# Three moves in the first block of a one-core retention and Mish kernel: outer products ahead of scores, two weight casts to other engines, three weight sums later

## The chip, the cores and the metric

The kernel runs on one core of one Trainium2 chip. The metric is the device time of one execution, in microseconds (us); where several runs are compared, their median. The engines are called as the profile calls them: PE is TensorE's matmul row and PEld its weight loads, DVE is VectorE, ACT is ScalarE, POOL is GpSimd, SP is SyncE, which here only issues DMAs.

## The reference

There are two stages. The first is a linear recurrence for each batch and head (4 batches, 8 heads, 768 tokens, 64 wide), the second a feed-forward layer on its output (3072 tokens, 512 wide, 2048 inside):

```
state = gamma[h] * state + outer(k[t], v[t])      # 64x64 for each batch and head
y[t]  = scale * q[t] @ state
x     = y, heads side by side                     # 3072 x 512
h     = x @ w_in                                  # 512 x 2048
g     = h * tanh(softplus(h))                     # Mish
out   = g @ w_out                                 # 2048 x 512
```

All inputs and the output are float32; the kernel computes its matmuls in float16.

## The kernel before

**The recurrence in chunks.** The kernel cuts the tokens into 24 chunks of 128. Within a chunk the recurrence is a masked product: scores (k times q, L314 and L497), a mask (L321, L504, L565), and the product of the masked scores with v (the "present" part, L374). Between chunks it is a state: outer products of k and v (L333, L483) are added to the state so far and decayed (L345), and the state times q is the "past" part (L381). Both parts add up in PSUM and are copied out as `xt`, the transposed input of the second stage.

**Blocks.** The second stage works on blocks of chunks: the first block has 4 chunks (512 tokens), the other ten have 2 each. `first_block` is written out by hand: it holds the whole opening, in which inputs and weights arrive by DMA, and it is the function that the change edits, with `first_g2`, the second matmul of that block. From block 1 on, `g1_seven` (L820) and `seven` (L956) do the two matmuls with seven products in place of eight, which needs sums and differences of the weights (`win_sums`, L770, for w_in and `weight_sums`, L722 to L725, for w_out), of x (`x_sums`, L781 to L786) and of g (`g_sum`).

**Order of work.** The schedule is manual: every engine executes its instructions in the order in which the program issues them, and waits only on semaphores that the framework derives from the tiles. A list `late` holds closures for sums that aren't urgent; `some_late(n)` issues the next n of them at that place. `plan` says which extra work is issued behind the u-th group of the first block's first matmul (L687).

**The opening, chunks 2 and 3.** For this pair of chunks the program issues, in this order: the past part of chunk 1 (L381); the second halves of the scores and of the mask for the pair (L314, L321); the outer products of chunk 2 (L333) and its state (an identity matmul that adds the state so far, L343, and the decay, L345); the first-matmul groups u = 0 and 1 for the tokens of chunks 0 and 1 (L1057); the present part (L374), which reads the mask's output; the past parts of chunks 2 and 3 (L381), of which the last reads chunk 2's state; the cast of the second half of weight slice 0 (L206), and groups u = 2 and 3, which use that half.

**Weight slices.** w_in comes in four slices of 512 columns, each cast to float16 in two halves by `cast_win(s, half, engine)`: L206 on DVE or POOL, L204 on ACT. Slice 3 serves the groups u = 12 to 15; its second half serves u = 14 and 15.

**PSUM.** Two pools: `mm` has four buffers of one bank and `at` two buffers of two. The group u = 14 of L687 takes the `mm` buffer of group u = 10, which is free when ACT has computed the Mish of u = 10 (L703). At the start of block 1 (L820) the first two products on `mm` take the buffers of pair 0 of `first_g2`: the first is free after DVE's L1281, the third group of L820 (product "first", half 1) after ACT's L1286, which in the program waits for DVE's L1284. The product "fifth", half 0, waits for DVE's first L840.

**DVE and POOL in `first_g2`.** DVE's order there is: cast of w_out slice 2 (L216), L723, L724, L1183, L725, two L1247, L722, the fifth chunk's state L608, two masks L565, L723, L724, L1281, L725, L1284, then the sums of x. POOL's order is: a one-column copy that waits for L723 (`gate`, L427), two casts of q (L406), one of v (L423), two DMA issues (L418), two casts of v (L423), two DMA issues, a cast of q (L406).

Of the kernel before, what the change touches and what calls it, by code (L numbers as in the profile page):

```python
# [16 lines left out]
def kernel(  # L17
# [9 lines left out]
    nc = tc.nc  # L27
# [15 lines left out]
    NSL = 4  # L43
# [14 lines left out]
    def toks(c):  # L58
        return slice(c * HB, (c + 1) * HB)
# [83 lines left out]
    nload, late, early = [0], [], set()  # L143
    BRING = CPB
    stores = []
    last_ended, yet = [], []

# [49 lines left out]
    def cast_win(s, half, eng):  # L199
        src = wtmps["in", s]  # L200
        t = cpool.tile([P, NBP, TB // 2], FP16, name=f"win{s}_{half}")
        src = src[:, :, half * (TB // 2):(half + 1) * (TB // 2)]
        if eng is nc.scalar:
            nc.scalar.copy(t, src)  # L204
        else:
            eng.tensor_copy(t, src)  # L206
        wins[s, half] = t

    def cast_wout(s, f, on_act=False):
        if s not in wouts:  # L210
            wouts[s] = cpool.tile([P, FPS, d_model], FP16, name=f"wout{s}")
        dst, src = wouts[s][:, f], wtmps["out", s][:, f]
        if on_act:
            nc.scalar.copy(dst, src)
        else:
            nc.vector.tensor_copy(dst, src)  # L216
# [110 lines left out]
    def outer_first(s, chunks=(0, 1)):  # L327
        u_ps = {c: mmps.tile([P, HP, P], FP32, name="u_ps", tag="mm") for c in chunks}
        for i in range(HP):
            half, j = divmod(i, HP // 2)  # L330
            for r in range(R):
                for c in chunks:
                    nc.tensor.matmul(  # L333
                        u_ps[c][:, i], k16s[s][toks(c), half, r, 2 * j:2 * j + 2],
                        v16s[s, half][toks(c), r, 2 * j:2 * j + 2],
                        start=i == 0 and r == 0, stop=r == R - 1, skip_group_check=True)
        for c in chunks:
            us[2 * s + c] = u_ps[c]
# [46 lines left out]
    def xt_out(g, y):  # L385
        nc.scalar.copy(xts[0][:, g:g + 2], y)
# [47 lines left out]
    def at_tile():  # L434
        return atps.tile([P, 2, HP // 2, R, C], FP32, name="at", tag="at")
# [271 lines left out]
    def some_late(n):  # L707
        for _ in range(min(n, len(late))):
            late.pop(0)()
# [351 lines left out]
    def first_block():  # L1061
        qf = load_first_q()
        for s in range(2):
            for nm in "kv":
                for half in range(2):
                    load_two(nm, s, half)
        nload[0] = CPB
        load_weights()
        xts[0] = xtp.tile([P, CPB, HP, C], FP16, name="xt")

        at = at_tile()
        spin_wide(at, HP)
        spin_wide(at, HP)
        spin_wide(at, 2)
        tq = turn_first_q(qf, 0)
        spin(at, HP)
        first_q_out(0, tq, nc.scalar)
        tq = [tq, turn_first_q(qf, 1, True)]
        cast_two("k", 0, 0, True)
        turn_two(0, 0)  # L1080
        turned_two(0, 0)
        cast_two("k", 0, 1, True)
        turn_two(0, 1)
        first_q_out(1, tq[1], nc.vector)
        turned_two(0, 1)
        spin(at, HP)
        scores_half(0, 0, at)
        mask_half(0, 0, at)
        for half in range(2):
            cast_two("v", 0, half)  # L1090
        at = at_tile()
        spin(at, HP)
        scores_half(0, 1, at)
        mask_half(0, 1, at)
        cast_two("k", 1, 0)
        turn_two(1, 0)
        turned_two(1, 0)
        cast_two("k", 1, 1)
        outer_first(0)
        state_first(0)  # L1100
        at = at_tile()
        scores_half(1, 0, at)
        mask_half(1, 0, at)
        y = atps.tile([P, 2, HP, C], FP32, name="y_ps", tag="at")
        in_two = [y[:, c] for c in range(2)]
        present_first(0, in_two, range(HP))
        turn_two(1, 1)
        turned_two(1, 1)
        state_first(1)
        past_first(1, in_two)  # L1110
        xt_out(0, y)
        for half in range(2):
            cast_two("v", 1, half)
        cast_win(0, 0, nc.gpsimd)
        at = at_tile()
        scores_half(1, 1, at)
        mask_half(1, 1, at)
        y = [atps.tile([P, 2, HP, C], FP32, name="y_ps", tag="at")[:, 0] for _ in range(2)]
        outer_first(1, [0])
        state_first(2)  # L1120
        h_ps = [mmps.tile([P, 1, TB], FP32, name="h_ps", tag="mm") for _ in range(2)]
        for u in range(2):
            first_g1(h_ps[u], u, 0)
        present_first(1, y, range(HP))
        past_first(2, y)
        past_first(3, y)
        cast_win(0, 1, nc.vector)
        xt_out_by_two(2, y)
        for u in range(2, FPS):
            h_ps.append(mmps.tile([P, 1, TB], FP32, name="h_ps", tag="mm"))  # L1130
            first_g1(h_ps[u], u, 0)
        for u in range(FPS):
            first_g1(h_ps[u], u, 1)
            mish(0, u, h_ps[u])
        for s in range(1, NSL - 1):
            for half in range(2):
                cast_win(s, half, nc.vector)
            if s == 1:
                fourth_state()
            if s == 2:  # L1140
                late.extend(win_sums(0))
                some_late(8)
        room_for_sums()

        def more_sums():
            late.extend(win_sums(1))
            some_late(8)
            late.extend(weight_sums(0) + weight_sums(1))

        plan = {6: [(cast_win, NSL - 1, 0, nc.scalar)],  # L1150
                7: [(cast_win, NSL - 1, 1, nc.scalar), (more_sums,)],
                9: [(cast_wout, 0, slice(0, 3)), (cast_wout, 0, slice(3, 4), True), (room_for_more,),
                    (bring_first,)],
                10: [(some_late, 1)],
                12: [(g_sum, 1)],
                13: [(cast_wout, 1, slice(0, 3)), (g_sum, 2), (g_sum, 3)],
                16: [(load_more,)]}
        for u in range(FPS, NFB):
            g1(0, u)
            for fn, *args in plan.get(u + 1, ()):  # L1160
                fn(*args)
        first_g2()
        hsnaps.append(gp.tile([P, 4, TB], FP32, name="hsnap", tag="g0"))

# [20 lines left out]
    def first_g2():  # L1185
# [33 lines left out]
        for p in pairs:  # L1219
            mm(pe[p], sm(p, 1), t(1), True)  # L1220
            nc.scalar.copy(m5[p], pe[p])
        cast_wout(2, slice(0, 2))
        cast_wout(2, slice(2, 4), True)
        some_late(1)
        gate(tmats[0][:, 1, 0, :1])
# [28 lines left out]
        for p in pairs:  # L1254
            mm(px[p], a(p, 1, 1), b(1, 0))
            if p == 0:
                outer_fifth(CPB)
        cast_wout(3, slice(2, 4), True)
        decay_of_fifth()
        scores(CPB)  # L1260
# [158 lines left out]
```

## Time and profile before

| | us |
|---|---|
| median of 3 runs | 190.82 (190.69 to 191.54) |
| the profiled execution: its own time | 190.88 |
| the profiled execution: its span, first to last instruction | 189.0 |
| PE busy within the span | 182.5 |
| DVE busy | 155.6 |
| ACT busy | 126.8 |
| POOL busy | 95.3 |

The profile comes from one execution. Its span begins with the first instruction of the program and ends with the last; 1.9 us of the execution's time lie around it. A row of the timeline gives the start, the duration, the engine, the line of the kernel, the operation, its output and inputs, the shapes and the number of instructions merged into the row; in square brackets stands how long the engine was idle before it and what ended that idle time. Rows of pipelined instructions overlap a little.

### The profile page before, as it was taken

The page shows a single profiled execution, that of the slowest core. Times are in us where ns is not written, and L with a number is a line of the kernel's source. Part 1 is how long each engine was busy: PE and PEld are TensorE (multiplying, and loading weights), DVE is VectorE, ACT ScalarE, POOL GpSimd, SP SyncE. Part 2 cuts the span into 40 slices and gives each one's busy share as a digit, 9 for nine tenths or more (in the row PEclk, how much of TensorE's full clock was granted, in tenths as well). Part 3 has the DMA queues.
Part 4 walks back from the last instruction along what each step waited for, and adds up shares of the span by engine and source line. Part 5 has one row for each costly group of instructions (what it writes and reads, how often), then busy time and mean ns, then how long its engine had stood idle before and what let it go on. Part 6 is the DMA issues. An engine that isn't in the chain of part 4 may idle for free.

```text
span 189.0 us, 7724 instructions
## 1 busy us (share of the span) xinstructions
PE 182.5 (97%) x3283; PEld 155.8 (82%) x3283; DVE 155.6 (82%) x329; ACT 126.8 (67%) x249; POOL 95.3 (50%) x135
## 2 busy tenths in 40 slices
PE   7789999999999999999999999999999999999992
PEld 3457546975988988988988988988988989989981
DVE  3997899879899699797897897797897897796662
ACT  3462599385883983983983984974874974965960
POOL 6570107696878937924935925916916913000000
PEclk9999999999999999999999999999999999999999
DMA  5999999999999999999998995999996984300203
GB/s 165 351 368 405 404 407 279 278 248 134 151 192 251 180 285 210 208 219 177 167 194 146 188 187 158 197 195 120 178 203 117 148 144 59 114 0 17 101 0 111
DMA packets 95521, 36.17 MB, mean 191 GB/s; under 512 B 82560, under 2 KB 88960, under 8 KB 95488
## 3 DMA queue, kind: packets, MB, share of 16 engines
q1 hardware_dynamic: 74112, 32.78, 75.3%
q0 software_dynamic: 21088, 2.62, 22.4%
q8 instruction: 25, 0.41, 0.9%
q10 hardware_dynamic: 288, 0.30, 0.4%
q14 instruction: 8, 0.07, 0.1%
HBM read 27.30 MB, written 6.29 MB: 178 GB/s over the span
## 4 chain that ended last, share of the span: by engine, by line
PE 91%; DVE 3%; DMA 2%; POOL 1%; issue 1%; ACT 0%; SPq 0%; DVEq 0%; POOLq 0%
PE h_ps L820 34%; PE o_ps L956 32%; PE h_ps L687 6%; PE o_ps L1210 5%; DMA qfirst<-in_q_dram 2%; PE h_ps L1057 2%; PE o_ps L1275 2%; PE y_ps L532 2%; PE u_ps L483 2%; PE at L497 2%; DVE am L321 2%; PE y_ps L543 2%; POOL qfirst L249 1%; DVE osb L977 1%; PE at L314 0%
## 5 line engine op out<-in xcount | busy, mean ns | idle before, releaser
L840 DVE TENSOR_TENSOR hsum<-h_ps,hsnap 128x512 f32<-128x512 f32 x60 | 38.5, 685 | 10.1 <-ACT hsnap L830 6.6
L830 ACT COPY hsnap<-h_ps 128x512 f32<-128x512 f32 x60 | 32.1, 589 | 10.3 <-PE h_ps L820 10.1
L820 PEld LDWEIGHTS <-wsum 128*128 128x128 f16 x640 | 36.2, 98 | 0.1
L835 ACT ACTIVATE g<-hsum 128x512 f16<-128x512 f32 x60 | 34.6, 643 | 0.6 <-DVE hsum L840 0.2
L956 PEld LDWEIGHTS <-gsum 128*128 128x128 f16 x320 | 30.4, 98 | 3.7
L820 PE MATMUL h_ps<-xsum,wsum 128*128 128x128 f16 x480 | 30.2, 220 | 0.0
L956 PE MATMUL o_ps<-tmat,gsum 128*128 128x256 f16 x240 | 29.5, 273 | 0.0
L820 PEld LDWEIGHTS <-win 128*128 128x128 f16 x480 | 28.2, 98 | 0.9
L418 POOL DMA_DIRECT2D qk<-in_k_dram x36 | 27.5, 777 | 0.0
L956 PEld LDWEIGHTS <-g 128*128 128x128 f16 x248 | 22.7, 98 | 2.6
L406 POOL TENSOR_TENSOR qk<-qf,qvs 128x512 f16<-128x512 f32 x20 | 22.1, 1106 | 0.0
L956 PE MATMUL o_ps<-wout,g 128*128 128x256 f16 (+1 forms) x168 | 20.8, 268 | 0.0
L423 POOL TENSOR_TENSOR v<-vf,qvs 128x512 f16<-128x512 f32 x20 | 20.7, 1060 | 0.0
L820 PE MATMUL h_ps<-xt,win 128*128 128x128 f16 x320 | 19.6, 220 | 0.0
L550 ACT COPY hsum<-y_ps 128x512 f32<-128x512 f32 x9 | 5.3, 585 | 18.3 <-PE y_ps L543 18.3
L977 DVE TENSOR_TENSOR osb<-o_ps,snap 128x256 f32<-128x256 f32 (+1 forms) x32 | 13.0, 413 | 5.0 <-PE o_ps L956 2.4
L597 POOL TENSOR_TENSOR stc<-suc,gcv 128x256 f16<-128x256 f32 x15 | 9.9, 662 | 13.6 <-DVE suc L592 13.6
L427 POOL COPY gate<-gsum 128x1 f16<-128x1 f16 x10 | 1.9, 186 | 26.8 <-DVE gsum L927 26.8
L965 ACT COPY snap<-o_ps 128x256 f32<-128x256 f32 x31 | 11.4, 371 | 5.4 <-PE o_ps L956 5.0
L820 PE MATMUL h_ps<-xsum,win 128*128 128x128 f16 x160 | 12.3, 220 | 0.0
L820 PE MATMUL h_ps<-xt,wsum 128*128 128x128 f16 x160 | 12.2, 220 | 0.0
L835 ACT ACTIVATE g<-h_ps 128x512 f16<-128x512 f32 x20 | 12.0, 599 | 0.0
(144 smaller groups left out, 309.4 us busy)
## 6 DMA issues: line engine op xcount, KB each, us to landing
vf<-in_v_dram SPq DMA_DIRECT2D x24, 256.0 KB, 6.2
out_dram<-osb SPq DMA_DIRECT2D x22, 256.0 KB, 2.9
qf<-in_q_dram SPq DMA_DIRECT2D x20, 256.0 KB, 5.3
wi<-in_moe_w_in_dram SPq DMA_DIRECT2D x3, 1024.0 KB, 10.5
wt<-in_moe_w_out_dram SPq DMA_DIRECT2D x3, 1024.0 KB, 9.6
qk<-in_k_dram POOLq DMA_DIRECT2D x36, 64.0 KB, 5.1
qfirst<-in_q_dram SPq DMA_DIRECT2D x2, 512.0 KB, 4.3
kf<-in_k_dram SPq DMA_DIRECT2D x4, 256.0 KB, 4.9
```

What stands on the lines that cost most here:

```text
L406: nc.gpsimd.tensor_tensor(by_head(g, room16(g)[0]), by_head(0, loaded[g][0]), f.broadcast_to((P, 2, HP, D)), op=ALU.mult)
L418: nc.gpsimd.dma_start(room16(g)[1][:, x::2], src[:, HP * x:HP * x + HP])
L423: nc.gpsimd.tensor_tensor(room16(g)[2], loaded[g][2], vs.unsqueeze(2).broadcast_to((P, H, D)), op=ALU.mult)
L597: by.tensor_tensor(stcs[g], sus.pop(g), decay, op=ALU.mult)
L687: nc.tensor.matmul(h_ps[:, j], win(s, f, bp), xt(blk, bp), start=(bp == 0), stop=(bp == NBP - 1))
L820: nc.tensor.matmul(h_ps[g][:, f], w(g, f, d), x(d), start=first and f == 0 and d == 0, stop=d == n - 1, skip_group_check=True)
L830: nc.scalar.copy(x, h_ps)
L835: nc.scalar.activation(gt[:, fb:fb + FPS, j * P:(j + 1) * P], h, AF.Mish, scale=inv_boost3)
L840: nc.vector.tensor_tensor(h, h_ps, x, op=ALU.add)
L956: nc.tensor.matmul(t, x(f), w(f)[:, c], start=first and f == 0, stop=f == n - 1, skip_group_check=True)
L965: nc.scalar.copy(x[:, c], t)
L977: nc.vector.tensor_tensor(dst[:, c], t, plus[:, c], op=ALU.add)
```

## The change

It has four parts, all in the first block.

1. The outer products of chunk 2 (`outer_first(1, [0])`) are issued ahead of the second half of the scores of chunks 2 and 3, and no longer behind their mask.
2. The second half of weight slice 0 is cast by POOL, right behind the first half, and no longer by DVE behind the past parts.
3. The second half of weight slice 3 is cast by DVE and no longer by ACT.
4. Of the eight sums of w_in that `more_sums` issues, five stay. The last three wait in a new list, `later`: one is issued in `first_g2` between the two casts of w_out slice 2, and two between the fifth chunk's outer products and the cast of the second half of w_out slice 3.

```diff
-    last_ended, yet = [], []
+    last_ended, yet, later = [], [], []
...
         cast_win(0, 0, nc.gpsimd)
+        cast_win(0, 1, nc.gpsimd)
+        outer_first(1, [0])
         at = at_tile()
         scores_half(1, 1, at)
         mask_half(1, 1, at)
         y = [atps.tile([P, 2, HP, C], FP32, name="y_ps", tag="at")[:, 0] for _ in range(2)]
-        outer_first(1, [0])
         state_first(2)
...
         past_first(2, y)
         past_first(3, y)
-        cast_win(0, 1, nc.vector)
         xt_out_by_two(2, y)
...
             late.extend(win_sums(1))
-            some_late(8)
+            some_late(5)
+            later.extend(late)
+            late.clear()
             late.extend(weight_sums(0) + weight_sums(1))
 
         plan = {6: [(cast_win, NSL - 1, 0, nc.scalar)],
-                7: [(cast_win, NSL - 1, 1, nc.scalar), (more_sums,)],
+                7: [(cast_win, NSL - 1, 1, nc.vector), (more_sums,)],
...
         cast_wout(2, slice(0, 2))
+        later.pop(0)()
         cast_wout(2, slice(2, 4), True)
...
                 outer_fifth(CPB)
+        later.pop(0)()
+        later.pop(0)()
         cast_wout(3, slice(2, 4), True)
```

## The prediction, made before the change was run

> **What bounds the kernel now.** I read the table of windows first, then the timelines of the engines in the opening, then DVE and POOL side by side up to the start of block 1.
>
> ```profile
> core 0: us, PE busy (x) PEld busy (x) DVE busy (x) ACT busy (x) POOL busy (x), PEclk, DMA share, GB/s
> 13.60:20.00 6.40, 6.30 (x114) 5.03 (x114) 4.98 (x8) 3.04 (x6) 0.92 (x1) 1.00 1.06 405
> 20.00:30.60 10.60, 10.56 (x54) 4.71 (x50) 9.98 (x23) 8.45 (x15) 2.34 (x3) 1.00 1.06 396
> ...
> 47.00:185.00 138.00, 138.00 (x2787) 127.20 (x2785) 115.41 (x241) 99.00 (x200) 70.63 (x99) 1.00 0.98 155
> ```
>
> From 47 to 185 us PE has no gap, at full clock. So what the first 47 us give or take reaches the end unchanged, and only PE's stalls there count. The edit reaches three of them: one at 13.7, one at 28.8, and a place at 47 where there is none yet.
>
> **Parts 1 and 2, the opening.** PE, then DVE and POOL:
>
> ```profile
> 13.00 0.39 PE L381 MATMUL y_ps<-qfirst_t,st 128*128 128x128 f16 x4
> 13.70 0.42 PE L314 MATMUL at<-qfirst_t,qkt 64*64 64x128 f16 x16 [0.32 <-DVE am L321]
> 14.05 0.62 PE L333 MATMUL u_ps<-v,qk 64*128 64x128 f16 x8
> 14.60 0.39 PE L343 MATMUL u_ps<-st,ident 128*128 128x512 f16 x1
> 14.83 1.04 PE L1057 MATMUL h_ps<-xt,win 128*128 128x256 f16 x8
> 15.80 0.64 PE L374 MATMUL y_ps<-am,v 64*64 64x128 f16 x32
> 16.37 0.62 PE L381 MATMUL y_ps<-qfirst_t,st 128*128 128x128 f16 x8
> 16.83 2.87 PE L1057 MATMUL h_ps<-xt,win 128*128 128x256 f16 x24
> ```
>
> ```profile
> 13.57 0.68 DVE L345 TENSOR_TENSOR st<-u_ps,gcm 128x512 f16<-128x512 f32 x1
> 14.17 1.22 DVE L321 TENSOR_TENSOR am<-at,tri_first 128x1024 f16<-128x1024 f32 x1
> 15.31 0.68 DVE L345 TENSOR_TENSOR st<-u_ps,gcm 128x512 f16<-128x512 f32 x1
> 15.91 0.68 DVE L206 CAST win<-wi 128x1024 f16<-128x1024 f32 x1
> ```
>
> ```profile
> 11.36 2.08 POOL L288 TENSOR_TENSOR v<-vf,qvs 128x512 f16<-128x512 f32 x2 [0.96 <-DMA vf<-in_v_dram]
> 13.48 1.04 POOL L206 CAST win<-wi 128x1024 f16<-128x1024 f32 x1
> ```
>
> Eight L381 take 0.46 (16.37 to 16.83), so the four at 13.00 have issued at 13.23; the change of tile shape costs about 0.10 (eight L1057 at 0.11 would take 0.87, but L374 comes 0.97 behind). So the outer products start at 13.33. Their second half needs POOL's second v: done at 13.44, asked for at 13.6, no wait. Eight take 0.55 (14.05 to 14.60): the scores start at 13.88. The change therefore does not fill the gap for free: the scores come 0.18 later than at 13.70. They end at 14.30, the mask starts 0.05 behind, 14.35 instead of 14.17, and ends at 15.57.
>
> PE goes on: 16 scores to the next group take 0.35 (13.70 to 14.05), so L343 is due at 14.23 and waits for DVE's L345 (ends 14.25): 14.30. L1057 is due at 14.53 and waits for POOL's cast (ends 14.52): 14.60. Eight of them to L374: 0.97, so 15.57, and the mask, 15.57 plus 0.05, lets it run at **15.62 instead of 15.80: 0.18 gained**. DVE is now the limit here. Chunk 2's state ends at 16.17 and is asked for at 16.42.
>
> The cast on POOL costs 1.04 by its twin at 13.48 (0.68 on DVE). That twin ran beside L345 and the mask, as the new one does, and none of the three is longer for it. When its data are there:
>
> ```profile
> wt<-in_moe_w_out_dram SPq DMA_DIRECT2D x3, 1024.0 KB, 9.6
> ...
> wi<-in_moe_w_in_dram SPq DMA_DIRECT2D x2, 512.0 KB, 5.3
> ```
>
> The two halves of slice 0 land 5.3 after issue in the middle, and DVE's cast at 15.91 waited for nothing, so the second half landed before 15.91; about 14.8 by the DMAs' order. POOL ends between 15.6 and 16.95, I take 15.9; groups u = 2, 3 ask at 16.65. Free, or at worst 0.3. DVE loses a cast in front of L390, where it idled anyway; POOL has nothing else until 21. SP may issue w_out's slice 0, which takes slice 0's buffer, some 0.7 sooner, but with the DMAs at a share of 1.06 it queues behind slice 3: nothing.
>
> The Trainium skill, "TensorEngine Tiling (Array Packing)", Key Properties, says that a change of tiling mode drains TensorE. The trace shows less than a full drain: L343 starts at 14.60, while the last L333 is shown until 14.67. By the rule the scores and the mask would come about 0.07 later and 0.11 be left of the 0.18.
>
> **Part 3, ACT.**
>
> ```profile
> 28.84 1.39 PEld L687 LDWEIGHTS <-win 128*128 128x128 f16 x7 [0.32 <-issue]
> ```
>
> ```profile
> 25.28 1.04 ACT L204 CAST win<-wi 128x1024 f16<-128x1024 f32 x1
> ...
> 27.18 0.63 ACT L214 CAST wout<-wt 128x512 f16<-128x512 f32 x1
> 27.69 3.68 ACT L703 ACTIVATE g<-h_ps 128x512 f16<-128x512 f32 x7
> ```
>
> Seven loads in 1.39 are 0.215 apart with 0.12 between them; before u = 14 it is 0.32: a stall of **0.20**. The group waits for the Mish of u = 10, the second of the seven, ended at about 28.79. Without the cast at 25.28, L214 can start when its DMA lands: issued behind slice 0's casts (15.91 + 0.68 = 16.6), plus 9.6: 26.3 instead of 27.18. The Mish of u = 10 ends at 27.9, asked for at 28.45: the stall goes. Slice 3's half on DVE is ready before 26.6, asked for at 28.4.
>
> **Part 4 and DVE's load.** DVE's stretch from 25.86 to 28.79:
>
> ```profile
> 25.86 0.42 DVE L770 TENSOR_TENSOR wsum<-win 128x512 f16<-128x512 f16 x1
> ...
> 28.79 0.95 DVE L216 CAST wout<-wt 128x1536 f16<-128x1536 f32 x1
> ```
>
> Eight sums take 2.93; three fewer save 1.1, the cast adds 0.6 (0.68 less the overlap), so DVE runs 0.5 ahead, and PE with ACT 0.38. The first late sum (0.34) falls ahead of L723:
>
> ```profile
> 34.05 0.69 DVE L723 TENSOR_TENSOR tmat<-wout,tmat 128x1024 f16<-128x1024 f16 x1 [0.25 <-ACT wout L214]
> ...
> 35.87 1.53 DVE L725 TENSOR_TENSOR tmat<-wout,tmat 128x1024 f16<-128x1024 f16 x1
> ```
>
> ```profile
> 35.35 2.95 POOL L406 TENSOR_TENSOR qk<-qf,qvs 128x512 f16<-128x512 f32 x2
> ```
>
> 0.25 of idle plus 0.12 of lead cover it. Behind L723 nothing moves against PE. The other two are not so placed. These rows (all times below on the clock of before; subtract 0.38):
>
> ```profile
> 40.20 0.43 DVE L608 TENSOR_TENSOR suc<-u_ps,stc 128x256 f32<-128x256 f32 x1 [0.36 <-PE u_ps L604]
> 41.08 2.36 DVE L565 TENSOR_TENSOR am<-at,tri 128x1024 f16<-128x1024 f32 x2 [0.45 <-PE at L469]
> 43.35 0.68 DVE L723 TENSOR_TENSOR tmat<-wout,tmat 128x1024 f16<-128x1024 f16 x1
> 43.95 0.68 DVE L724 TENSOR_TENSOR tmat<-wout,wout 128x1024 f16<-128x1024 f16 x1
> ...
> 45.15 0.93 DVE L725 TENSOR_TENSOR tmat<-wout,tmat 128x1024 f16<-128x1024 f16 x1
> 46.23 0.42 DVE L1284 TENSOR_TENSOR osb<-o_ps,osb 128x256 f32<-128x256 f32 x1
> ```
>
> ```profile
> 40.81 2.06 POOL L423 TENSOR_TENSOR v<-vf,qvs 128x512 f16<-128x512 f32 x2
> 42.80 1.55 POOL L418 DMA_DIRECT2D qk<-in_k_dram  x2
> 44.36 1.17 POOL L406 TENSOR_TENSOR qk<-qf,qvs 128x512 f16<-128x512 f32 x1
> ```
>
> ```profile
> 46.79 0.41 ACT L1286 COPY osb<-o_ps 128x256 f32<-128x256 f32 x1
> 46.89 1.95 PE L820 MATMUL h_ps<-xt,win 128*128 128x128 f16 x32
> ```
>
> By time alone, two sums of 0.34 in an idle stretch of 0.45 cost DVE 0.2, which its idle time ahead of L1284 nearly takes up. But DVE's sums of two operands in SBUF and POOL's work exclude each other: L725 at 35.87 takes 1.53 instead of 0.69, ending 0.55 behind POOL's first L406, and each L406 takes 1.48, against 1.03 for an L423 of the same shape (two in 2.06). Of a held instruction's time 0.14 is over before it needs its turn (0.69 less the 0.55 that L725 still needs); so a held sum needs 0.28 more and a held cast 0.90. POOL, which came (35.35) while an earlier sum ran, went ahead of L725 (35.87): they take turns. The masks, with one operand in PSUM, run at 1.18 beside POOL undisturbed.
>
> Now the two sums: the first runs 40.55 to 40.97, POOL's L423 comes at 40.81, the second sum would start at 40.89. POOL is ahead by **0.08**, so the second sum waits until 41.87 and ends at 42.15. The mask starts at 42.07 instead of 41.08; the second L723 at 44.34, the second L724 at 44.94. POOL's L406, itself 0.18 late, comes at 44.54, between them, and holds L724: it ends at 46.47 (45.02 + 0.90 + 0.55). Then L1281 ends at 47.07, L725 at 47.68, L1284 starts at 47.59 and ends at 48.01, ACT's L1286 ends at 48.46. Before, L1284 ended at 46.65 and L1286 at 47.20, and PE asked for it at 47.78 (third group of L820, 46.89 + 2 x 0.447): a slack of 0.53.
>
> PE then: the first group waits for L1281, 47.12 instead of 46.89 (0.23); the third, now due at 48.01, waits until 48.51 (0.50); and the first L840, behind the sums of x, comes about 0.15 late for the product "fifth". **Stall: 0.88.** Bounds: 0 (the sum goes ahead of POOL; nothing is taken away here, so it can't gain) and 1.4 (L1284's whole lateness, 48.01 less 46.65, without the slack). I take 0.88, since the order at 35.35 is the nearest row. The sums themselves are due only in the products of half 1 behind 49.5, long after 42.15.
>
> The Trainium skill, "SBUF — State Buffer", Who interferes with whom, speaks against this part: a VectorE instruction with two SBUF inputs and a GpSimd one that reads SBUF block each other fully, the one behind waiting. The rows above agree (1.53, 1.48). Without the rule the sum would be that of the first rival.
>
> **Sum**, from the profiled execution, 190.88: less 0.18, less 0.20, plus 0.88: 191.38; the median lies 0.06 under that execution, so **191.3**.
>
> **Rivals.**
> - *The sums run ahead of POOL.* If POOL's chain, which hangs on L723, is 0.08 later against PE than I have it (DVE's part of the opening 0.15 late would do, since the late sum ahead of L723 leaves next to no idle time), or DVE keeps its turn for both sums, the masks are 0.15 late and PE never waits: 190.82 - 0.38 = 190.4. For: the margin is small. Against: both chains hang on PE by fixed durations.
> - *Slower: the lateness feeds itself in block 1.* DVE has 115.4 busy of 138; if, arriving 1.3 late, its sums of x and g meet POOL's casts again in wrong turns, PE stalls once more by the 0.85 of such a turn: 192.2. It decides if DVE has not caught up by about 53 us. For: the mechanism is the same and both engines are busy there. Against: PE has moved 0.88 with it, some 0.4 is left to catch up, and DVE has gaps.
> - *It doesn't do what it says.* POOL's v comes 0.3 later, the outer products wait for it with the scores behind them, and the mask takes the gain of the opening; w_out's first slice lands over 0.5 later, and PE's stall at 28.8 stays: 190.8. For: both hang on DMAs, of which one execution shows one landing each. Against: it needs both.
>
> **Chances.** Forecast 0.50 (own range 191.0 to 191.6), sums first 0.30 (190.2 to 190.6), slower by feedback 0.09, nothing gained or lost 0.08, gains that I do not see, under 189.9, 0.03. The range 190.2 to 191.6 leaves out the feedback, the unseen gains and the edges. 0.5% is 0.95 us, about what a measurement of this kernel can tell from no change: forecast, first rival and the third lie within it. Faster 0.04, same 0.86, slower 0.10.
>
> **What would show it.** Right: L333 at about 13.3 ahead of L314, L374 at 15.6; no idle time of PEld ahead of u = 14; the second late sum of 0.42 stretched to over 1.2 beside L423; L724 stretched to 1.5; PE waiting at L820 for ACT's L1286. Wrong: both late sums at 0.42 and L820 at 46.5 without a gap (first rival); L374 at 15.8 or later (third); or PE gaps behind 53 us (second).

## The result, and the profile after

The changed kernel takes **191.87 us** (median of 10 executions, 191.58 to 192.91) and the kernel before, run beside it, 190.97 (190.69 to 191.61): a ratio of 1.0054, 95% interval 1.0032 to 1.0077, so about 1.0 us slower. The forecast was 191.3 with a range up to 191.6: the sign was right, the time lies above the range. The profiled execution took 191.79, with a span of 190.0; against the span before that is 1.0 more.

Three views answer to those of before. First the opening, TensorE's row and then those of VectorE and GpSimd (start, duration, engine, line; in brackets the idle time ahead of it):

```profile
13.34 0.62 PE L333 MATMUL u_ps<-v,qk 64*128 64x128 f16 x8
13.88 0.42 PE L314 MATMUL at<-qfirst_t,qkt 64*64 64x128 f16 x16
14.32 0.38 PE L343 MATMUL u_ps<-st,ident 128*128 128x512 f16 x1
14.62 1.05 PE L1057 MATMUL h_ps<-xt,win 128*128 128x256 f16 x8
15.60 0.67 PE L374 MATMUL y_ps<-am,v 64*64 64x128 f16 x32
```

```profile
14.35 1.22 DVE L321 TENSOR_TENSOR am<-at,tri_first 128x1024 f16<-128x1024 f32 x1
```

```profile
14.88 1.04 POOL L206 CAST win<-wi 128x1024 f16<-128x1024 f32 x1 [0.32 <-DMA wi<-in_moe_w_in_dram]
```

The outer products stand at 13.34, the scores at 13.88, the mask at 14.35 and L374 at 15.60: each within 0.02 of the forecast (13.33, 13.88, 14.35, 15.62). The same is true of ACT and of the group u = 14:

```profile
26.29 0.62 ACT L214 CAST wout<-wt 128x512 f16<-128x512 f32 x1
26.81 2.54 ACT L703 ACTIVATE g<-h_ps 128x512 f16<-128x512 f32 x5
```

```profile
27.61 2.26 PEld L687 LDWEIGHTS <-win 128*128 128x128 f16 x11
```

Eleven weight loads run without a gap where seven started behind 0.32 of idle time: TensorE is 0.37 ahead of the kernel before from 28.5 to 44 us in this trace. Then come VectorE, GpSimd and TensorE around the start of block 1:

```profile
40.18 0.68 DVE L770 TENSOR_TENSOR wsum<-win,win 128x512 f16<-128x512 f16 x1
40.79 1.26 DVE L770 TENSOR_TENSOR wsum<-win,wsum 128x512 f16<-128x512 f16 x1
41.98 2.34 DVE L565 TENSOR_TENSOR am<-at,tri 128x1024 f16<-128x1024 f32 x2
...
44.84 1.52 DVE L724 TENSOR_TENSOR tmat<-wout,wout 128x1024 f16<-128x1024 f16 x1
46.29 0.68 DVE L1286 TENSOR_TENSOR osb<-o_ps,osb 128x512 f32<-128x512 f32 x1
...
47.49 0.41 DVE L1289 TENSOR_TENSOR osb<-o_ps,osb 128x256 f32<-128x256 f32 x1
```

```profile
39.08 1.57 POOL L418 DMA_DIRECT2D qk<-in_k_dram  x2
40.65 2.30 POOL L423 TENSOR_TENSOR v<-vf,qvs 128x512 f16<-128x512 f32 x2
42.90 1.56 POOL L418 DMA_DIRECT2D qk<-in_k_dram  x2
44.46 1.35 POOL L406 TENSOR_TENSOR qk<-qf,qvs 128x512 f16<-128x512 f32 x1
```

```profile
43.96 0.82 PE L640 MATMUL y_ps<-am,v 128*64 128x128 f16 x16
...
45.40 1.47 PE L1280 MATMUL o_ps<-wout,g 128*128 128x512 f16 x6
47.02 1.07 PE L820 MATMUL h_ps<-xt,win 128*128 128x128 f16 x16
48.35 1.13 PE L820 MATMUL h_ps<-xt,win 128*128 128x128 f16 x16 [0.27 <-ACT osb L1291]
...
52.75 0.61 PE L820 MATMUL h_ps<-xt,wsum 128*128 128x128 f16 x8
```

TensorE's rows of before at the same places:

```profile
44.33 0.64 PE L640 MATMUL y_ps<-am,v 128*64 128x128 f16 x16
...
45.58 1.47 PE L1275 MATMUL o_ps<-wout,g 128*128 128x512 f16 x6
...
51.83 0.61 PE L820 MATMUL h_ps<-xt,wsum 128*128 128x128 f16 x8
```

The changed kernel's L1286, L1289, ACT's L1291 and TensorE's L1280 are L1281, L1284, L1286 and L1275 of before. The chain of the forecast is there: the second late sum is stretched to 1.26 beside L423, L724 to 1.52 beside L406, and TensorE's third group at L820 waits for ACT. What differs is that the first late sum is stretched too, 0.68 instead of 0.42, and that TensorE is 0.92 behind at 52.75, where before it stood at 51.83: with the 0.37 that it was ahead, **1.29 of stall instead of 0.88**.

### The profile page after: what moved, and what is told of

It is laid out like the page before. It is cut to its first block, busy times and chain, and to the rows that moved or that the text cites. A ratio compares the mean times of both kernels' runs of the same rounds, so it can differ in the third digit from the quotient of the medians.

```text
span 190.0 us, 7725 instructions
## 1 busy us (share of the span) xinstructions
PE 182.3 (96%) x3283; PEld 155.3 (82%) x3283; DVE 157.2 (83%) x329; ACT 126.2 (66%) x248; POOL 95.3 (50%) x136
## 4 chain that ended last, share of the span: by engine, by line
PE 87%; DVE 4%; DMA 3%; SPq 2%; issue 1%; ACT 1%
PE h_ps L820 33%; PE o_ps L956 32%; PE h_ps L687 6%; PE o_ps L1212 4%; DMA kf<-in_k_dram 3%; PE h_ps L1057 2%; PE y_ps L532 2%; PE at L497 2%; PE u_ps L483 2%; SPq L270 2%; PE y_ps L543 2%; DVE am L565 1%; DVE tmat L724 1%; PE y_ps L374 1%; DVE osb L977 1%
## 5 line engine op out<-in xcount | busy, mean ns | idle before, releaser
L840 DVE TENSOR_TENSOR hsum<-h_ps,hsnap 128x512 f32<-128x512 f32 x60 | 38.6, 684 | 9.7 <-ACT hsnap L830 6.8
L830 ACT COPY hsnap<-h_ps 128x512 f32<-128x512 f32 x60 | 32.1, 589 | 9.8 <-PE h_ps L820 9.7
L820 PEld LDWEIGHTS <-wsum 128*128 128x128 f16 x640 | 36.2, 98 | 0.2 <-issue 0.2
L835 ACT ACTIVATE g<-hsum 128x512 f16<-128x512 f32 x60 | 34.6, 642 | 0.7 <-DVE hsum L840 0.3
L820 PE MATMUL h_ps<-xsum,wsum 128*128 128x128 f16 x480 | 30.2, 219 | 0.0
L820 PEld LDWEIGHTS <-win 128*128 128x128 f16 x480 | 28.2, 98 | 1.7 <-DVE osb L1286 0.6
L418 POOL DMA_DIRECT2D qk<-in_k_dram x36 | 27.6, 781 | 0.0
L406 POOL TENSOR_TENSOR qk<-qf,qvs 128x512 f16<-128x512 f32 x20 | 22.3, 1116 | 0.0
L423 POOL TENSOR_TENSOR v<-vf,qvs 128x512 f16<-128x512 f32 x20 | 21.0, 1074 | 0.0
L820 PE MATMUL h_ps<-xt,win 128*128 128x128 f16 x320 | 19.9, 219 | 0.4 <-ACT osb L1291 0.3
L820 PE MATMUL h_ps<-xsum,win 128*128 128x128 f16 x160 | 12.3, 220 | 0.0
L820 PE MATMUL h_ps<-xt,wsum 128*128 128x128 f16 x160 | 12.2, 219 | 0.0
L835 ACT ACTIVATE g<-h_ps 128x512 f16<-128x512 f32 x20 | 12.0, 599 | 0.0
```

Source lines behind the costliest of these rows:

```text
L406: nc.gpsimd.tensor_tensor(by_head(g, room16(g)[0]), by_head(0, loaded[g][0]), f.broadcast_to((P, 2, HP, D)), op=ALU.mult)
L418: nc.gpsimd.dma_start(room16(g)[1][:, x::2], src[:, HP * x:HP * x + HP])
L423: nc.gpsimd.tensor_tensor(room16(g)[2], loaded[g][2], vs.unsqueeze(2).broadcast_to((P, H, D)), op=ALU.mult)
L820: nc.tensor.matmul(h_ps[g][:, f], w(g, f, d), x(d), start=first and f == 0 and d == 0, stop=d == n - 1, skip_group_check=True)
L830: nc.scalar.copy(x, h_ps)
L835: nc.scalar.activation(gt[:, fb:fb + FPS, j * P:(j + 1) * P], h, AF.Mish, scale=inv_boost3)
```

## The experiments

The theory: the two late sums at 40 us cost the whole stall, by turns with GpSimd's casts, and all else of the change keeps its 0.37 us. The rivals: that TensorE's early arrival alone upsets the order at 44 us, that the sum ahead of L723 does it, or that VectorE has no room for the cast. All times are medians of the 6 to 12 executions of five rounds beside the kernel before; the ratio with its 95% interval is worked out from the same runs and isn't the quotient of the two medians. Each kernel's rows come from one of its executions, which need not be at the median. The kernels of each heading ran on one chip. The edits under the first heading are to the kernel before, the others to the changed kernel.

### The parts alone (kernel before: 190.94)

**Parts 1 and 2 alone.** 

> Parts 1 and 2 alone: outer products of chunk 2 ahead of the scores, slice 0's second half cast by POOL. Theory (the loss of 0.9 us is all in the turns of DVE and POOL that the two late sums set off at 40 us): L374 at 15.6 instead of 15.8, PE then 0.18 early up to 28.6 us, where the wait for ACT ahead of u = 14 grows by the 0.18 or stays 0.20, and no new gap at 47 us: 190.6 to 190.8 against 190.8 of before, ratio 0.999 to 1.000. Rival (it is enough for PE to arrive early at 44 us for DVE and POOL to fall into the wrong turns): a gap at L820 of 0.5 or more, 191.2 to 191.6.

```diff
         cast_win(0, 0, nc.gpsimd)
+        cast_win(0, 1, nc.gpsimd)
+        outer_first(1, [0])
...
-        outer_first(1, [0])
         state_first(2)
...
-        cast_win(0, 1, nc.vector)
```

Measured: 190.88, ratio 1.0006 (0.9986 to 1.0025). L374 runs at 15.58, so TensorE is 0.22 early; all of it goes at u = 14:

```profile
28.84 1.39 PEld L687 LDWEIGHTS <-win 128*128 128x128 f16 x7 [0.54 <-issue]
```

The idle time ahead of the group grew from 0.32 to 0.54 and its start stays at 28.84. The opening alone gains nothing: ACT's order, which part 3 relieves, decides when this group starts. No new gap at 47 us: the first rival falls.

**Part 3 alone.** 

> Part 3 alone: slice 3's second half cast by VectorE, all eight sums left where they were. Theory: the 0.20 us ahead of u = 14 goes, DVE is 0.6 later up to 31 us (w_out's slice 0 cast 0.6 later, asked for at 30.4, slice 1 later too); if DVE catches up in its idle time between 31 and 40 us, 190.6, and the late order at 40 us is that of before. Rival (DVE has no room for the cast): PE waits for DVE's casts or sums between 30 and 36 us by up to 0.5, 190.8 to 191.2.

```diff
-                7: [(cast_win, NSL - 1, 1, nc.scalar), (more_sums,)],
+                7: [(cast_win, NSL - 1, 1, nc.vector), (more_sums,)],
```

Measured: 191.37, ratio 1.0025 (1.0009 to 1.0041). The 0.21 at u = 14 is gained, then 0.56 lost up to 31.8: the rival named the right wait, and its price is above the rival's range. With parts 1 to 3 together TensorE waits at the same place; that row stands below.

**Part 4 alone**, with the cast on ACT. 

> Part 4 alone: three sums later, the cast left on ACT, the opening as before. Theory (the two sums at 40 us cost the 1.3 us of stall in turns with POOL): the wait of 0.20 ahead of u = 14 stays, and PE loses 1.0 to 1.3 us between 44 and 53 us: 191.8 to 192.1, ratio 1.005 to 1.007. Rival (the lateness comes with the early start of the w_out casts or with the cast on DVE): the sums fit in DVE's idle time, 190.8 to 191.1.

```diff
-    last_ended, yet = [], []
+    last_ended, yet, later = [], [], []
...
-            some_late(8)
+            some_late(5)
+            later.extend(late)
+            late.clear()
...
+        later.pop(0)()
         cast_wout(2, slice(2, 4), True)
...
+        later.pop(0)()
+        later.pop(0)()
         cast_wout(3, slice(2, 4), True)
```

Measured: 192.52, ratio 1.0085 (1.0053 to 1.0117), above the forecast. VectorE's sums and GpSimd's casts:

```profile
40.47 0.49 DVE L770 TENSOR_TENSOR wsum<-win,win 128x512 f16<-128x512 f16 x1
40.88 2.27 DVE L770 TENSOR_TENSOR wsum<-win,wsum 128x512 f16<-128x512 f16 x1
43.07 2.34 DVE L565 TENSOR_TENSOR am<-at,tri 128x1024 f16<-128x1024 f32 x2
```

```profile
40.74 2.12 POOL L423 TENSOR_TENSOR v<-vf,qvs 128x512 f16<-128x512 f32 x2
```

Here the second sum waits through both casts (2.27), not one. The masks come 2.0 late and TensorE loses 0.89 at L640 already. Part 4 costs this without any other part. That DVE and POOL take turns, as the forecast had it, doesn't hold.

**Parts 1 to 3, all eight sums early.** 

> Parts 1 to 3, with part 4 undone: all eight sums early, nothing of them at 33 and at 40 us. Theory: PE keeps the 0.37 us that the opening and the wait at u = 14 gave, less what DVE's cast costs between 28 and 31 us (bounds 0 and 0.3): 190.4 to 190.8, ratio 0.998 to 1.000; masks and L723 at 41 to 44 us in the order of before. Rival (an early PE alone breaks the order at 44 us): 191.3 or more, with L724 or L725 stretched to 1.5 and a gap at L820.

 Its edit is the first two of the diffs above together.

Measured: 191.28, ratio 1.0011 (0.9993 to 1.0029).

```profile
31.77 1.05 PE L1210 MATMUL o_ps<-tmat,gsum 128*128 128x256 f16 x8 [0.35 <-DVE gsum L1177]
```

The lead of 0.35 turns into 0.33 of lag: 0.15 goes at 30.37, where TensorE waits for VectorE's L216, and 0.53 here, since eight sums and the cast put DVE's L1177 at 31.02 to 31.70 and TensorE asks for it at about 31.2. The theory had allowed 0.3 at most for the cast. The order behind it, at 40 to 47 us, is that of before. So part 3 needs part of part 4.

### The place of the late sums (kernel before: 190.89)

**The two sums of 40 us moved to 50 us.** 

> The changed kernel, but the last two late sums leave the place at 40 us: VectorE issues them in block 1 behind the second pair of osb sums (about 50.3 to 51.0 us), where it idled 0.5. Theory (the whole loss comes from these two sums at 40 us): the masks start with TensorE again, L820 comes without a wait, PE stays 0.37 early and block 1 costs 0 to 0.2: 190.4 to 190.6, ratio 0.997 to 0.999. Rival (the first late sum and the early PE set POOL's casts against L724 or L725 anyway): a gap of 0.4 or more at L820, 191.0 to 191.6.

```diff
-        later.pop(0)()
-        later.pop(0)()
...
-            "at3": [(end_first,), (load_to, a + 3)],
+            "at3": [(end_first,), (later.pop(0),), (later.pop(0),), (load_to, a + 3)],
```

Measured: 192.30, ratio 1.0070 (1.0046 to 1.0093). The cause was right: L820 starts at 46.65 without a wait, 0.37 ahead of the changed kernel. The price of the new place was wrong:

```profile
50.34 1.09 DVE L770 TENSOR_TENSOR wsum<-win,win 128x512 f16<-128x512 f16 x1
51.36 1.48 DVE L770 TENSOR_TENSOR wsum<-win,wsum 128x512 f16<-128x512 f16 x1
```

```profile
49.92 1.55 POOL L418 DMA_DIRECT2D qk<-in_k_dram  x2
51.48 2.25 POOL L423 TENSOR_TENSOR v<-vf,qvs 128x512 f16<-128x512 f32 x2
```

The first is held by GpSimd's DMA issues, the second by its cast, and TensorE, which needs them at once here, waits 0.78 for the second and 0.20 for VectorE's L840 behind it. This run's rival falls: with no sum at 40 us there is no gap at L820.

**The two sums behind the masks.** 

> The changed kernel, with the same two sums behind the two masks instead of ahead of them. Theory (what costs is the hold by POOL, at whatever place it falls): the masks are on time, so the 0.17 of PE at L640 goes; the sums push L723, L724 and the osb sums by 0.7, POOL's L406 comes at 44.3 between them and holds one by 0.8: stall at L820 of 0.6 to 1.0, 191.0 to 191.5. Rival (the cost is that of the masks' lateness alone): no stall, 190.4 to 190.6.

```diff
-        later.pop(0)()
-        later.pop(0)()
         cast_wout(3, slice(2, 4), True)
...
         mask(CPB + 1)
+        later.pop(0)()
+        later.pop(0)()
         some_late(2)
```

Measured: 191.87, ratio 1.0053 (1.0029 to 1.0078). Both sums run at 0.44 and 0.41 and the masks are on time, but they push L724 to 44.28, behind GpSimd's L406 at 44.19: L724 takes 1.55 and TensorE's third group waits for ACT. At 47 us TensorE is 0.50 ahead of the changed kernel. So the push of L724 costs by itself, with masks on time; that the masks' lateness is all of it is ruled out. The rest of the time goes at 83 us, taken up below.

**GpSimd's cast of v ahead of its DMA issues.** 

> The changed kernel, with POOL's cast of v of chunk CPB+1 ahead of its two DMA issues of k (39.1 to 40.65 us in the changed kernel), so that no cast of POOL starts between 40.2 and 41 us. Theory (the second late sum loses its 0.85 to the cast L423): both late sums take 0.42 or, beside the DMA issues, up to 0.7 each, the masks start at 41.0 to 41.3, the stall shrinks from 1.29 to 0.3 or less, unless L724 meets L406 as before: 190.4 to 190.9. Rival (the hold is not by the cast but by anything that POOL does): 191.6 to 191.9 as the changed kernel.

```diff
-        bring_k(CPB + 2)
         cast_v(CPB + 1)
+        bring_k(CPB + 2)
```

Measured: 191.19 (190.65 to 192.96), ratio 1.0022 (1.0002 to 1.0041). The sums take 0.68 and 0.41, the masks start at 41.23, L724 takes 0.68 and ACT is no longer waited for at L820. In their place stands the DMA that was issued 1.56 later:

```profile
46.49 0.31 PE L483 MATMUL u_ps<-v,qk 64*64 64x64 f16 x15 [1.09 <-DMA qk<-in_k_dram]
```

The theory's hold by the cast is confirmed: without a cast behind the first sum, the second runs free. The time lies above the forecast. The traced execution took 192.08, 0.9 above the median, so the wait for this DMA is longer in it than in most of them.

**Six sums early, two at 40 us.** 

> The changed kernel, with the first of the three late sums back among the early ones (six early, two late at 40 us). Theory (this sum, ahead of L723, makes POOL's chain 0.2 late against PE, and with it the meeting at 40 us): L723 starts 0.2 to 0.35 sooner, POOL's cast at 40.65 comes sooner and holds the first of the two sums, not the second; w_out's casts 0.34 later, PE's product with the sums of g at 31 us asks for L1179 with 0.2 to spare: no stall there. Stall at 44 to 52 us of 1.0 to 2.0: 191.5 to 192.4. Rival (the first late sum is what costs): 190.4 to 190.9.

```diff
-            some_late(5)
+            some_late(6)
...
         cast_wout(2, slice(0, 2))
-        later.pop(0)()
```

Measured: 192.26, ratio 1.0071 (1.0053 to 1.0088). The time was as expected, not the way: the second sum, 0.14 behind L423 as in the changed kernel, waits through both casts, 2.27 as with part 4 alone.

### Fewer sums at 40 us (kernel before: 191.10)

**Six early, one ahead of L723, one at 40 us.** 

> The changed kernel with six sums early, one ahead of L723 and only one at 40 us. Theory (the wait comes from the second of two sums at 40 us, which arrives 0.14 behind POOL's cast L423; the first is held by 0.26 at most beside the DMA issue L418 and ends at 40.8 to 40.9): the masks start 0.1 to 0.2 late at most, L724 is ahead of POOL's L406 as in the kernel before, no wait at L820, PE stays 0.37 early: 190.4 to 190.7, ratio 0.997 to 0.999. Rival (any sum at this place sets the order behind it wrong): L724 stretched to 1.5 and a wait at L820, 191.0 to 191.5.

```diff
-            some_late(5)
+            some_late(6)
...
-        later.pop(0)()
         later.pop(0)()
         cast_wout(3, slice(2, 4), True)
```

Measured: 191.14, ratio 1.0008 (0.9991 to 1.0024). At 40 us the theory holds: one sum of 0.68, masks at 41.36, L724 0.68, no wait at L820. But the sixth early sum costs:

```profile
32.47 3.70 PE L1212 MATMUL o_ps<-wout,g 128*128 128x256 f16 x32 [0.25 <-DVE wout L216]
```

TensorE loses 0.42 there, since L216 ends at 32.42: it took 1.43 instead of 0.95 beside GpSimd's DMA issues L415.

**Six early, one ahead of L723, one at 50 us.** 

> The changed kernel with six sums early, one ahead of L723, the last in block 1 behind the osb sums at 50.3 us, none at 40 us. Theory (where a sum of two SBUF operands meets POOL, it is held by what POOL still has to do): nothing late up to 50 us; the one sum is held beside the DMA issues L418 from 50.35 to about 51.4 as the first of two was, TensorE's products that ask for it at 51.8 do not wait, the sums of h come 0.2 late: 190.4 to 190.8. Rival (block 1 has no room for any sum): a wait of 0.5 or more at 52 us, 191.0 or more.

```diff
-            some_late(5)
+            some_late(6)
...
-        later.pop(0)()
-        later.pop(0)()
         cast_wout(3, slice(2, 4), True)
...
-            "at3": [(end_first,), (load_to, a + 3)],
+            "at3": [(end_first,), (later.pop(0),), (load_to, a + 3)],
```

Measured: 191.10, ratio 0.9994 (0.9977 to 1.0010). The same 0.42 at 32 us; the sum at 50.80 takes 0.73 and delays nothing.

**Six early, two ahead of L723.** 

> The changed kernel with six sums early and the other two ahead of L723 at 33 us, none at 40 us. Theory (it is the place at 40 us that costs, not the number of sums): L723 and POOL's gate behind it come 0.1 to 0.35 later, VectorE still ends L725 before its idle time at 37.3 to 37.8 is used up, and POOL's casts at 40 us, later by as much, meet no sum: 190.4 to 190.7. Rival (POOL's chain hangs on L723, so its lateness costs wherever it comes from): L406 at 44.5 or later holds an osb sum or L725, a wait at L820 of 0.3 or more, 190.9 to 191.5.

```diff
-            some_late(5)
+            some_late(6)
...
         later.pop(0)()
+        later.pop(0)()
         cast_wout(2, slice(2, 4), True)
...
-        later.pop(0)()
-        later.pop(0)()
         cast_wout(3, slice(2, 4), True)
```

Measured: 191.68, ratio 1.0026 (1.0009 to 1.0043). On top of the 0.42, L723 at 34.83 makes GpSimd's L406 late, and TensorE's transposes (L453) wait for it: 0.32 more. The rival is right in the cause, not in the place (L820 starts without a wait): GpSimd's chain hangs on L723 and has no slack for a second sum.

**The changed kernel again.** 

> The changed kernel itself once more, for a second trace of it and more times. Theory (which of VectorE's second late sum and POOL's second cast L423 goes first at 41.76 us is settled by some ns, as three kernels in which the sum came 0.14 behind the first cast showed both orders): the sum takes 1.26 or 2.27, the masks start at 42.0 or 43.0; median 191.6 to 192.0. Rival (the order is fixed by the program): the same rows as in the first trace to within 0.05.

 No edit.

Measured: 192.60 (191.67 to 194.25), ratio 1.0074 (1.0048 to 1.0100). The median was expected at 191.6 to 192.0 and lies 0.6 above; the traced execution, 191.67, is the fastest of twelve, so its rows don't explain the median. Its trace has the second sum at 1.26 again, but nothing was settled between the two engines there. GpSimd's second cast had to wait for its data, and the sum had ended, at 41.83, before the cast started:

```profile
41.99 1.04 POOL L423 TENSOR_TENSOR v<-vf,qvs 128x512 f16<-128x512 f32 x1 [0.45 <-DMA vf<-in_v_dram]
```

So the other order at this place wasn't seen in the same program, and this trace doesn't speak for either. What did turn over is the pair of ten us before. VectorE and GpSimd in the first trace:

```profile
30.42 1.42 DVE L216 CAST wout<-wt 128x1536 f16<-128x1536 f32 x1
```

```profile
29.09 1.98 POOL L415 DMA_DIRECT2D qk<-in_k_dram  x2
```

and in the second:

```profile
30.41 0.95 DVE L216 CAST wout<-wt 128x1536 f16<-128x1536 f32 x1
```

```profile
29.09 2.75 POOL L415 DMA_DIRECT2D qk<-in_k_dram  x2
```

In one execution the cast waits for the DMA issues, in the other they wait for the cast. In the second trace the first late sum took 0.48, the masks started at 41.75 (forecast 41.70), and still TensorE's stall is 1.14.

### One sum in each of three places (kernel before: 191.12)

**One ahead of L723, one at 40 us, one at 50 us; five early.** 

> The changed kernel with its three late sums in three places: one ahead of L723 as it is, one at 40 us, the last in block 1 behind the osb sums at 50 us. Theory (the second sum at 40 us is the whole loss, and five early sums keep w_out's casts on time even where L216 is held): no wait at 32 us, none at L820, the last sum is held to 51.2 beside L418 and delays nothing: PE 0.25 to 0.37 early to the end, 190.4 to 190.7, ratio 0.997 to 0.999. Rival (a single sum at 40 us or the one in block 1 costs once PE is early): a wait of 0.4 or more at 44 to 53 us, 191.0 or more.

```diff
-        later.pop(0)()
         later.pop(0)()
...
-            "at3": [(end_first,), (load_to, a + 3)],
+            "at3": [(end_first,), (later.pop(0),), (load_to, a + 3)],
```

Measured: 191.06 (190.54 to 191.61), ratio 0.9999 (0.9984 to 1.0013).

```profile
40.17 0.68 DVE L770 TENSOR_TENSOR wsum<-win,win 128x512 f16<-128x512 f16 x1
40.77 2.34 DVE L565 TENSOR_TENSOR am<-at,tri 128x1024 f16<-128x1024 f32 x2
...
43.64 0.68 DVE L724 TENSOR_TENSOR tmat<-wout,wout 128x1024 f16<-128x1024 f16 x1
```

```profile
46.51 1.95 PE L820 MATMUL h_ps<-xt,win 128*128 128x128 f16 x32
...
51.45 0.61 PE L820 MATMUL h_ps<-xt,wsum 128*128 128x128 f16 x8
```

No wait up to 53 us: L820 at 46.51 instead of 46.89, the group that stood at 51.83 at 51.45. The whole stall is gone with the second sum at 40 us, and TensorE is 0.38 ahead of the kernel before. But the time is that of the kernel before, not the 190.4 to 190.7 expected: most of the lead is lost later, 0.20 of it at 82 us (L497), 0.05 at 87 and 0.12 at 101; 0.15 comes back at 133, and 0.16 is left at the last products.

**The same without parts 1 and 2.** 

> The same three places, cast of slice 3 by VectorE, but the opening as in the kernel before (parts 1 and 2 undone). Theory: only the 0.20 ahead of u = 14 is gained: 190.6 to 190.8, 0.1 to 0.2 above the kernel with the opening. Rival (the opening's gain is lost again by the time that it reaches u = 14): the same time as with it.

 Its edit is the one above with the first diff under "The parts alone" undone.

Measured: 190.83, ratio 0.9983 (0.9969 to 0.9998), the only one below the kernel before, by an interval that all but reaches 1. With the opening the median is 0.23 higher, not 0.1 to 0.2 lower; the two intervals overlap, so that the opening costs is not shown, only that its gain doesn't show in the time. Nor does the trace, of an execution of 190.96, show where 0.3 us would be gained: its lead of 0.22 is lost, and 0.08 more, at these products, which in the kernel before start at 53.83 and take 0.43:

```profile
53.75 0.60 PE L497 MATMUL at<-qkt 64*64 64x64 f16 x32
```

**The last sum behind the masks.** 

> The changed kernel with one late sum ahead of L723, one at 40 us and the last behind the masks, ahead of the second L723. Theory: the last sum pushes L724 by 0.34 to 43.9, still 0.2 to 0.5 ahead of POOL's L406, which is then the one that waits: no wait at L820, 190.4 to 190.7. Rival (L406 goes ahead of L724 whenever L724 is late): L724 stretched to 1.5, 0.4 to 0.9 of stall at L820, 190.9 to 191.4.

```diff
-        later.pop(0)()
         later.pop(0)()
         cast_wout(3, slice(2, 4), True)
...
         mask(CPB + 1)
+        later.pop(0)()
         some_late(2)
```

Measured: 191.19 (191.07 without one execution of 195.41), ratio 1.0012 (0.9989 to 1.0035). L724 starts at 44.34 and takes 0.69, GpSimd's L406 at 44.60 is the one that waits (1.31), and L820 starts without a gap, as the theory has it. The time again is not the 190.4 to 190.7 expected. In the profiled execution the first inputs came some 0.4 late, before any of the changed code; that explains this trace, not the median.

## Why the prediction was right or wrong

**Right: parts 1 to 3 and the mechanism of part 4.** The opening (0.18) and the wait at u = 14 (0.20) came as worked out, together 0.37. They weren't independent, though: the opening alone gave nothing, since it runs into the wait that part 3 takes away. The loss is the one forecast, at the place forecast, through the rows forecast: with one of the two sums taken from 40 us it is gone, in all four kernels that had one sum there.

**Wrong: the term "Stall: 0.88".** It measured 1.29, and 1.14 in the second trace. By its own steps:

| step | forecast | measured |
|---|---|---|
| masks' lateness and first group of L820 | 0.23 | 0.19 at L640 and 0.31 at L820 |
| third group, for ACT | 0.50 | 0.44 |
| what follows, up to 52 us | 0.15 | 0.08, 0.11 and 0.16 |
| sum | 0.88 | 1.29 |

Two things were mis-sized. The first late sum was taken at 0.42, as if it met nothing; it ran beside GpSimd's DMA issues L418 (to 40.65) and took 0.68, and all behind it came 0.27 later: second sum's end 42.05 (forecast 41.78), masks 41.98 (41.70), L1286's end 46.97 (46.70). Those 0.27 are the whole excess of the table's first line. And of the tail only one product's lateness was counted: L820 also waited for VectorE's L592 (0.08), L840 (0.11) and, at 52.7, the copy L830 on ACT (0.16). ACT was late there because its L835 had waited 0.28 for the first of those L840, so all three go back to VectorE's lateness. In the second trace, where the first sum took 0.48 and the masks were on time by the forecast, this tail (0.20 above the forecast) is most of the 0.26 that remains. The text named 1.4 as the upper bound, which gives 191.8, and then closed the range at 191.6: the bound should have set the edge. Of the 0.57 between forecast and time the stall makes 0.41; nearly all the rest is that the kernel before took 190.97 beside the changed one, not the 190.82 from which the forecast started.

The measured hold on that first sum goes against the Trainium skill, "SBUF — State Buffer", Who interferes with whom, which infers that a two-operand sum doesn't meet GpSimd's generation of descriptors. Here sums beside L418 took 0.68, 0.73 and 1.09 instead of 0.42, though not all of them did; the measurement decides. The part of that section by which a cast on VectorE and GpSimd's descriptor writing block each other, whoever is first, is what L216 and L415 show (1.42 beside 1.98, or 0.95 beside 2.75).

**Wrong: "Behind L723 nothing moves against PE".** The late sum ahead of L723 was to be covered by idle time. In the first trace L216 was held to 31.84, so L723 started at 33.90 without any idle time, 0.22 later than 0.37 ahead of 34.05 would be, and GpSimd's chain with it. In the second trace it started at 33.67 with 0.17 of idle, as forecast. The kernel's order at this point changes from one execution to the next.

**Not shown right: "they take turns".** The second sum came 0.14 behind L423 in the changed kernel, with part 4 alone and with six early sums; it went ahead of the second cast once and behind it twice, and in the changed kernel's second trace the cast wasn't ready to compete. That the rule gave the right row here was luck. The total was hardly touched: behind two casts TensorE waits earlier, at L640, and L724 then misses L406.

**Wrong in general: "what the first 47 us give or take reaches the end unchanged".** A loss mostly did, or grew: 0.92 at 53 us is 0.80 at the last products in the changed kernel, and 0.39 becomes 1.11 with both sums behind the masks. A lead mostly didn't. The kernel with one sum in each place leads by 0.38 at 53 us and by 0.16 at the end. VectorE's last sums of the output, first before, then there:

```profile
184.47 1.18 DVE L977 TENSOR_TENSOR osb<-o_ps,snap 128x256 f32<-128x256 f32 x4 [0.39 <-PE o_ps L956]
```

```profile
184.31 1.18 DVE L977 TENSOR_TENSOR osb<-o_ps,snap 128x256 f32<-128x256 f32 x4 [0.39 <-PE o_ps L956]
```

Both spans are 189.0 all the same: behind these sums the span runs on for 3.3 us in the trace of before and for 3.5 in this one. The same 0.2 is part of the 1.0 between the changed kernel's span and that of before (its last sums start at 185.27, 0.80 late). Why it differs is open.

The place where most of the lead goes is named by the kernel with both sums behind the masks, in TensorE's row:

```profile
82.28 0.32 PE L497 MATMUL at<-qkt 64*64 64x64 f16 x16
83.19 0.32 PE L497 MATMUL at<-qkt 64*64 64x64 f16 x16 [0.59 <-DMA qkt<-qk]
```

and in its chain from 70 to 84 us:

```profile
76.33 6.82 DMA qkt<-qk
...
83.19 0.32 PE at L497 x16
```

The second half of these products waits for a transpose by DMA, 6.82 behind its issue on SP. In the leading kernel the same 32 products take 0.65 instead of 0.45:

```profile
81.55 0.65 PE L497 MATMUL at<-qkt 64*64 64x64 f16 x32
```

Its timeline names no releaser there, but its DMA view does: the transpose issued at 75.09 landed 6.7 later, at 81.8, and the second half of the products started at 81.88. In the kernel before it was issued at 74.87 and landed after 5.8, over a microsecond before it was needed. The kernel without parts 1 and 2 lost 0.18 in the same way at 54 us: its transpose, issued at 49.31, took 4.7, to 54.0, where the second half started at 54.03; in the kernel before it took 4.1. So TensorE's lead did not make these transposes land sooner. Why they take longer in one trace than in another, whether a lead is lost to DMAs in general, and why the times of most kernels, that of before too, spread over 0.9 us and more, wasn't tried.

**The rivals.** *The sums run ahead of POOL* (190.4): no trace shows it, and where the loss is absent the times were 190.8 to 191.1, not 190.4. *The lateness feeds itself*: no further stall of that size behind 53 us; the changed kernel is 0.92 behind there and 0.80 from 133 us to its last products. *It doesn't do what it says*: it did.

## What to carry to other kernels

Where two engines hold each other, the price of moving an instruction is set by what the other engine does in the new place, its DMA issues included: look there for each instruction moved, not only for the one that collides by the clock. A place that has room for one more instruction need not have room for two. And a lead on a full engine was worth only as much as the slack of the transfers that it met later, while a delay was mostly kept here. Look up, too, where in the spread of its times the traced execution lies, before its rows are taken to explain a median.

## What the runs showed of the hardware

- In all eight traces in which a late sum came in the last 0.5 us of GpSimd's two DMA issues L418, it ended 0.21 to 0.23 behind their end, and so took 0.48 to 0.68 instead of 0.42. Sums that came earlier in the same two issues took 0.41 to 0.44 or 0.73 to 1.09, and when they came doesn't tell which: 0.71 behind the start of the issues one ran free (0.41, both sums behind the masks), 0.42 behind it another was held (1.09, both sums at 50 us).
- The order of VectorE's L216 and GpSimd's L415 differed between two executions of one program. GpSimd's two casts went ahead of a waiting sum in two kernels and let it in between them in a third, with the sum 0.14 behind the first cast in all three.
- In eleven traces with the new order of the opening, one of the matmuls of L1057 starts at 17.5 to 17.6 in six and at 17.7 in five, with nothing in the rows to explain it; in those five TensorE is only 0.26 ahead at u = 14, where the others that have part 3 are 0.35 to 0.44 ahead. The changed kernel's first ten times lie in two groups (191.58 to 191.94, 192.55 to 192.91), and both its traces are of executions of the lower group, whose stall is about the same. Both causes stay open.
